# The second layer's weights converted during the first layer's last block, with new costs in the list that orders the instructions

## The chip, the cores and the metric

The kernel runs on one core of a Trainium2 chip. The metric is the time of one execution on the device in microseconds (us), the median of several runs. Five engines with queues of their own matter here: TensorE (PE in the profile; PEld is its loading of weights), VectorE (DVE), ScalarE (ACT), GpSimd (POOL) and SyncE (SP), which here does nothing but issue DMAs.

## The reference, cut to what matters

```python
scores = scale * np.matmul(q, k.transpose(0, 1, 3, 2))        # 4 x 8 heads, 576 x 576, head width 64
cum = np.cumsum(np.log(np.clip(f, 0.0001, 1.0)), axis=-1)
scores = np.where(causal, -1e9, scores + cum[:, :, :, None] - cum[:, :, None, :])
attn = softmax(scores)
x = (attn @ v).transpose(0, 2, 1, 3).reshape(2304, 512)
h = x @ moe_w_in                                              # 512 -> 2048
x = (h * np.clip(h + 3.0, 0.0, 6.0) / 6.0) @ moe_w_out        # 2048 -> 512
h = x @ moe2_w_in
g = np.where(h >= 1, h, np.where(h <= -1, 0.0, (h + 1) ** 2 / 4))
return (g @ moe2_w_out).astype(np.float32)
```

An attention with a decay, and two dense layers of width 2048 over 2304 tokens. The four weight matrices arrive as 64-bit floats.

## The kernel before

**Work.** Attention goes over 4 batches and pairs of heads, the first 256 queries of a batch first, then the other 320. For a tile of 128 queries, `u_scores` makes scores in PSUM (tile `sc`), `softmax` adds the decay and takes minimum and exponential (`dec`, `dm`, `prob`), `u_norm` divides, `u_trans` transposes the probabilities through TensorE (`pt`), `u_out` multiplies by the values (`av`). `av` uses half of TensorE's columns (the profile shows the tile 128\*64); its last chunk of keys has 64 rows only (64\*64). `dec` is loaded from `ncum` in DRAM into one of two buffers.

**Layers.** Both dense layers go over blocks of tokens: five of layer 1 (512, 512, 512, 256, 512 wide) and five of layer 2. A block has 16 steps, one for each chunk of 128 hidden units. A step is 12 matmuls of `hp` (`moe_h`, weights `w[0]`), the activation on ACT and DVE (`u`, `g`), and 12 matmuls of `o` (`moe_o`, weights `w[1]`), two steps later. 12, because operands are split into a rounded part and a rest, and three of the products are taken. Attention is interleaved with blocks 0 to 3 of layer 1; what a block needs of it must be done before the block. Block 4 of layer 1 (steps 64 to 79) is the first without attention.

**Weights.** A raw half chunk (512 KB, `wraw`, three buffers) is turned into 32-bit floats in the tile `wr` (two buffers) by one ACT and four DVE instructions (`w_split`, L431 to L442), then split into the rounded part and the rest (ACT and DVE) in a slot `w`. There are 9 slots for each of the two matrices, and 16 from step 64 on, when attention's buffers are free. Layer 1's chunks are split once, written to `wf` in DRAM (`w_keep`) and loaded again where they don't stay. Layer 2's chunks go another way: between steps 17 and 62 (`PRE`, by width) they are loaded raw, converted, and the float is written to `wf` by a DMA that POOL issues (L447); in block 4 it comes back by a load of 256 KB (L416) and only then is split.

**Order.** The program is written in one order, and `plan` replaces it: `graph` gives each instruction its dependences and a cost, `schedule` runs a list over them (the engine and instruction that can begin first goes first), and each engine gets its row. A DMA costs bytes over `bw`, plus fixed times. All loads and stores but POOL's share one queue on SP, in that row's order. The tile `wr` also holds the parts that block 5's inputs are added from (`part`, L806 to L809) and layer 2's output.

Of the kernel before, what the change touches and what calls it, by code (L numbers as in the profile page):

```python
# [42 lines left out]
LAG = 2  # L43
GO = 0
XT = 11
PRE = (17, 62)
WRAW = 3
AHEAD = 60000
LEAD = (1, 1, 1, 1, 1, 1)
# [44 lines left out]
def graph(nc, homes, follows, held=()):  # L94
# [95 lines left out]
    for k in range(n):  # L190
        if eng[k] == "PE":
            last = k
        elif last is not None and type(ops[k]).__name__ == "InstDMACopy":
            if any(x[0].startswith(held) for x in info[k][1]) if held else False:
                deps[k].add(last)

    DMA = "DMA"
    cost, late, kind = [0.0] * n, [0.0] * n, [""] * n
    for k, i in enumerate(ops):
        t, (ins, outs) = type(i).__name__, info[k]  # L200
        e = eng[k]
        o = outs[0] if outs else None
        m = max([x[4] for x in ins + outs] or [1])
        psum = any(x[5] for x in ins)
        if t == "InstDMACopy":
            parts = (o[2] - o[1]) if homes.get(o[0], ("", bass.MemoryType.DRAM))[1] != bass.MemoryType.DRAM else P
            cost[k] = 420 if e == "SP" else 1100
            late[k] = 4.0 * o[4] * parts
            kind[k] = DMA
        elif e == "PE":  # L210
            cols = o[4]
            if str(i.ins[0].dtype).endswith("float32r"):
                c = max(cols, 64) / 2.4 + 13
            elif "pt" == o[0][:2]:
                c = 109
            else:
                c = 1.7 * cols if "sc" == o[0][:2] else max(120, cols * 0.82)
            cost[k], late[k] = c, 172
        elif e == "Activation":
            late[k] = 30  # L220
            cost[k] = (200 + 0.7 * m if psum else 215 + 0.83 * m) - 95 + (190 if len(outs) > 1 else 0)
            late[k] = 95 + 34
        elif e == "DVE":
            if t == "InstCustomDveAnt":
                c = 165 + 1.0 * m + 85
            elif t == "InstTensorTensor" or psum or t == "InstTensorCopy":
                c = 160 + 1.04 * m
            elif t == "InstTensorScalarPtr" and len(ins) < 2:
                c = 155 + 0.52 * m
            elif t == "InstTensorScalarPtr":  # L230
                c = 160 + 1.04 * m
                if len([x for x in ins if x[4] > 1]) < 2:
                    c = 155 + 0.52 * m
# [7 lines left out]
    return dict(eng=eng, deps=deps, users=users, slots=slots, nuses=nuses, first=first,  # L241
                where={x: (h[0], h[2]) for x, h in homes.items()}, cost=cost, late=late, kind=kind), ops, sets


def schedule(g, bw=330.0, fixed=3000.0, small=150.0):
    n, eng = len(g["eng"]), g["eng"]
    succ, left = [[] for _ in range(n)], [len(d) for d in g["deps"]]
    for k, d in enumerate(g["deps"]):
# [28 lines left out]
            t, need[tag] = max(t, f[m]), m + 1  # L277
        return t

    server = 0.0  # L280
    for _ in range(n):
        best = None
        for e in engines:
            for k in avail[e]:
                t = when(k)
                if t is not None:
                    c = (max(t, free[e]), k)
                    if best is None or c < best:
# [43 lines left out]
def tile_kernel(  # L332
# [27 lines left out]
    def bank(name):  # L360
# [2 lines left out]
        return p.tile([P, 512], F32, tag="ps", name=name)  # L363

    att = pool("att", 2)

    x2d = [dram.tile([DM, NT if x == 0 else T1[0]], F32, name=f"x2d{x}") for x in range(2)]
    wf = [
        [dram.tile([P, 2, 4, P] if c < NCH else [P, 4, P], F32, name=f"wf{c}_{x}") for x in range(2)]
        for c in range(2 * NCH)  # L370
    ]
    ncum = dram.tile([B * H, S], F32, name="ncum")
    wsb = [[wpool.tile([P, 2, 4, P], F32R, name=f"w{x}_{s}") for s in range(SLOTS[x])] for x in range(2)]
# [33 lines left out]

    def w_load(kind, c, half, s):
        if kind == "raw":
            raw = att.tile([P, 4 * P, 2], I32, tag="wraw", name="wraw", bufs=WRAW)  # L410
            nc.sync.dma_start(out=raw, in_=w[c // NCH, c % NCH, :, 8 * P * half:8 * P * half + 8 * P])
            return raw
        if kind == "parts":
            nc.sync.dma_start(out=wsb[half][s].bitcast(F32), in_=wf[c][half])
        else:
            nc.sync.dma_start(out=wsb[half][s][:, 1].bitcast(F32), in_=wf[c][half])  # L416

    def w_split(kind, c, half, s, raw):
        if kind == "parts":
            return  # L420
# [15 lines left out]
        nc.vector.tensor_scalar(  # L436
            out=t, in0=t, scalar1=5, scalar2=2, op0=ALU.logical_shift_left, op1=ALU.logical_shift_right
        )
        nc.vector.scalar_tensor_tensor(  # L439
            out=t, in0=hw, scalar=-1073741824, in1=t, op0=ALU.bitwise_and, op1=ALU.bitwise_or  # L440
        )
        nc.vector.scalar_tensor_tensor(  # L442
            out=t, in0=lw, scalar=29, in1=t,
            op0=ALU.logical_shift_right, op1=ALU.bitwise_or,
        )
        if s is None:
            nc.gpsimd.dma_start(out=wf[c][half], in_=r)  # L447
        else:
            hi, lo = wsb[half][s][:, 0], wsb[half][s][:, 1]
            rounded("a", hi, r)  # L450
            rest("v", lo, r, hi)

    def w_keep(c, half, s):
        nc.sync.dma_start(out=wf[c][half], in_=wsb[half][s].bitcast(F32))
# [218 lines left out]
    def u_trans(n, x):  # L673
# [3 lines left out]
        pr = pairs[d["p"]]  # L677
        if "pt" not in pr:
            pr["pt"] = att.tile([P, 4, 2, S - QA], F32, tag="pt", name="pt", bufs=1)
            if pr["half"]:  # L680
                pr["pt4"] = att.tile([D, 2, W4], F32, tag="pt4", name="pt4", bufs=1)
        pt = pr["pt"]
        t = bank("pt")

# [27 lines left out]
            rounded("a", pt[:, :, :, QA:S - QA], t.rearrange("p (c h n) -> p c h n", c=4, h=2))  # L712
        else:
            tr(0, prob[4], 4 * P, D)
            rounded("a", pr["pt4"].rearrange("p h n -> p (h n)"), t[0:D, 0:P])

    def u_out(p):

# [387 lines left out]
```

## Time and profile before

| | |
|---|---|
| runs | 1041.9, 1036.1, 1035.82 us; median 1036.1 us |
| profiled execution | 1042.43 us, span 1040.7 us |
| mean granted clock of TensorE | 0.974 |
| busy: PE, DVE, ACT, POOL | 1002.5, 586.5, 527.0, 94.6 us |
| moved by DMA | 148.19 MB |

Busy times are unions of one engine's instructions. A busy PE can still run at the lower clock, 0.5 of the full one, or change between tile shapes. The profiled execution lies 0.6% above the median.

### The profile page before, as it was taken

How to read it: one execution, taken by the hardware profiler on the slowest of the kernel's cores; microseconds unless marked ns; L12 is line 12 of the kernel's file. 1: busy time of each engine (PE TensorE's matmuls, PEld its weight loads, DVE VectorE, ACT ScalarE, POOL GpSimd, SP SyncE). 2: the span in 40 equal slices, each digit the busy share in tenths (PEclk: the TensorE clock that was granted, in tenths of full speed). 3: DMA queues.
4: the chain of work that ended last, by engine and by line, in shares of the span. 5: the costliest groups of instructions: out<-in, count | busy, mean ns of one | idle time of the engine just before them, and what ended most of it. 6: DMA issues, size and time to landing. Idle time of an engine off the chain costs nothing.

```text
span 1040.7 us, 14773 instructions
## 1 busy us (share of the span) xinstructions
PE 1002.5 (96%) x5002; PEld 802.5 (77%) x5002; DVE 586.5 (56%) x1390; ACT 527.0 (51%) x1208; POOL 94.6 (9%) x223
## 2 busy tenths in 40 slices
PE   7889989999889999989899999999999999999998
PEld 5557767776667778768798888888888888888897
DVE  6889768899877765868654565423322322222232
ACT  5987656566655644756543444333333333333343
POOL 2111111111111110112010000101000000000000
PEclk7688989999999999999999999999999999999999
DMA  6665478867687897557958433201100100000010
GB/s 184 192 205 160 119 225 268 276 200 237 173 302 265 258 299 241 172 160 237 294 163 336 153 119 94 98 1 41 41 1 1 66 1 1 20 26 1 1 42 21
DMA packets 76364, 148.19 MB, mean 142 GB/s; under 512 B 12544, under 2 KB 35584, under 8 KB 76288
## 3 DMA queue, kind: packets, MB, share of 16 engines
q1 hardware_dynamic: 73728, 138.86, 42.6%
q0 software_dynamic: 2560, 8.39, 2.1%
q8 instruction: 39, 0.64, 0.2%
q14 instruction: 37, 0.30, 0.1%
HBM read 113.59 MB, written 33.63 MB: 141 GB/s over the span
## 4 chain that ended last, share of the span: by engine, by line
PE 80%; DMA 11%; DVE 4%; ACT 3%; issue 1%; SPq 0%; POOL 0%; DVEq 0%; POOLq 0%; ACTq 0%
PE hp L822 34%; PE o L872 19%; PE o L865 14%; DMA dec<-ncum 6%; DMA wraw<-in_w 4%; PE av L728 4%; PE pt L686 4%; PE sc L642 3%; PE sc L632 1%; DVE prob L593 1%; PE sc L617 1%; ACT prob L599 1%; DMA wf<-wr 1%; DVE wr L439 1%; ACT wr L431 0%
## 5 line engine op out<-in xcount | busy, mean ns | idle before, releaser
L822 PE MATMUL hp<-xt,w 128*128 128x512 f32 (+1 forms) x960 | 237.5, 383 | 1.7 <-DVE xt L386 0.6
L865 PE MATMUL o<-g,w 128*128 128x512 f32 (+1 forms) x960 | 233.7, 379 | 0.0
L822 PE MATMUL hp<-x,w 128*128 128x512 f32 (+1 forms) x960 | 210.0, 368 | 0.0
L872 PE MATMUL o<-w,g 128*128 128x512 f32 x864 | 209.2, 390 | 0.0
L822 PEld LDWEIGHTS hp<-x,w 128*128 128x128 f32 x960 | 169.3, 188 | 31.3
L822 PEld LDWEIGHTS hp<-xt,w 128*128 128x128 f32 x960 | 168.7, 193 | 31.8 <-issue 1.5
L865 PEld LDWEIGHTS o<-g,w 128*128 128x128 f32 x960 | 166.9, 190 | 28.3 <-issue 0.7
L872 PEld LDWEIGHTS o<-w,g 128*128 128x128 f32 x864 | 160.9, 188 | 33.2 <-ACT osb L887 0.7
L834 DVE SCALAR_TENSOR_TENSOR u<-hp,u 128x512 f32<-128x512 f32 (+1 forms) x80 | 51.1, 638 | 211.4 <-ACT u L833 211.1
L832 ACT ACTIVATE u<-hp 128x512 f32<-128x512 f32 (+1 forms) x80 | 44.4, 555 | 196.4 <-PE hp L822 196.4
L386 DVE TENSOR_TENSOR g<-u,g 128x512 fp32r<-128x512 f32 (+1 forms) x160 | 102.3, 640 | 69.2 <-PE o L872 35.0
L378 ACT ACTIVATE g<-u 128x512 fp32r<-128x512 f32 (+1 forms) x160 | 94.0, 589 | 77.2 <-DVE u L834 50.9
L599 ACT ACTIVATE prob<-prob,mx 128x128 f32<-128x128 f32 (+4 forms) x144 | 83.3, 579 | 54.5 <-DVE mx L593 54.1
L686 PE MATMUL pt<-ident,prob 128*128 128x128 f32 (+1 forms) x400 | 72.9, 297 | 17.1 <-DVE prob L671 13.3
L829 ACT ACTIVATE u<-hp 128x512 f32<-128x512 f32 (+1 forms) x80 | 44.3, 553 | 80.5 <-PE hp L822 80.0
L830 DVE SCALAR_TENSOR_TENSOR u<-u,hp 128x512 f32<-128x512 f32 (+1 forms) x80 | 50.4, 630 | 59.6 <-ACT u L829 59.2
L378 ACT ACTIVATE pt<-pt 128x512 f32<-128x512 f32 (+3 forms) x160 | 63.8, 434 | 34.1 <-PE pt L686 33.3
L686 PEld LDWEIGHTS pt<-ident,prob 128*128 128x128 f32 (+1 forms) x400 | 50.9, 149 | 36.3 <-DVE prob L671 15.4
L593 DVE CUSTOM_DVE_ANT_0 prob<-sc,dec 128x256 f32<-128x256 f32 (+1 forms) x112 | 58.6, 534 | 34.5 <-DMA dec<-ncum 15.2
L728 PE MATMUL av<-pt,vv 128*64 128x320 f32 (+3 forms) x448 | 59.6, 384 | 2.9 <-ACT pt L378 2.8
L728 PEld LDWEIGHTS av<-pt,vv 128*64 128x64 f32 (+1 forms) x448 | 28.7, 141 | 34.9 <-issue 10.1
L431 ACT ACTIVATE wr<-wraw 128x512 f32<-128x512 f32 x64 | 42.6, 667 | 18.6 <-DMA wraw<-in_w 14.1
(71 smaller groups left out, 899.5 us busy)
## 6 DMA issues: line engine op xcount, KB each, us to landing
wraw<-in_w SPq DMA_DIRECT2D x64, 512.0 KB, 7.2
w<-wf SPq DMA_DIRECT2D x40, 512.0 KB, 9.4
wf<-w SPq DMA_DIRECT2D x28, 512.0 KB, 6.8
dec<-ncum SPq DMA_DIRECT2D x45, 256.0 KB, 4.9
kraw<-in_k SPq DMA_DIRECT2D x64, 144.0 KB, 5.1
wf<-wr POOLq DMA_DIRECT2D x32, 256.0 KB, 5.6
w<-wf SPq DMA_DIRECT2D x32, 256.0 KB, 2.7
x2d<-osb SPq DMA_DIRECT2D x22, 256.0 KB, 6.5
```

Of the source, the lines that this page charges most:

```text
L378: nc.scalar.activation(out=out, in_=in_, func=AF.Copy)
L386: e.tensor_tensor(out=out, in0=in_, in1=hi.bitcast(F32), op=ALU.subtract)
L593: nc.vector.tensor_tensor_reduce(out=py[:, a:e], in0=s, in1=dc, scale=-0.125, scalar=mx[:, 2 * z:2 * z + 1] if x else 3.0e38, op0=ALU.add, ...
L599: nc.scalar.activation(out=py, in_=py, func=AF.Exp, scale=-1.0, bias=mx[:, 2 * z + x:2 * z + x + 1], accum_out=sm[:, z:z + 1],)
L686: nc.tensor.transpose(t[:nk, o:o + P], p[:, c:c + nk], ident)
L728: nc.tensor.matmul(t[y * D:(y + 1) * D, o:nq], lhsT=vv[:nk, y, c], rhs=rhs, start=c == 0, stop=c == nkc - 1,)
L822: nc.tensor.matmul(hp, lhsT=ws[:, a, k], rhs=x[:, bb, 0:w], start=(k == 0 and a == 0 and bb == 0), stop=(k == KD - 1 and bb == 1),)
L830: nc.vector.scalar_tensor_tensor(out=u, in0=u, scalar=6.0, in1=hp, op0=ALU.min, op1=ALU.mult)
L832: nc.scalar.activation(out=u, in_=hp, func=AF.Relu, bias=0.5, scale=0.5)
L834: nc.vector.scalar_tensor_tensor(out=u, in0=hp, scalar=1.0, in1=u, op0=ALU.max, op1=ALU.min)
L865: nc.tensor.matmul(o, lhsT=ws[:, a, k], rhs=gg[:, bb], start=(n and k % m == 0 and a == 0 and bb == 0), stop=(last and bb == 1 and k % m = ...
L872: nc.tensor.matmul(acc[j][k], lhsT=gg[:, bb, k * P:(k + 1) * P], rhs=ws[:, a].rearrange("p k n -> p (k n)"), start=(n and a == 0 and bb == ...
```

## The change

Layer 2's chunks no longer pass through DRAM. Their raw halves are loaded from step 65 on, two halves every two steps (`LATE`), at the latest two steps before use, into `wraw` buffers in the memory that attention left (`rawp`), and converted and split straight into freed slots. The 32 writes by POOL and the 32 loads of 256 KB are gone, and the "whole" split with them. Besides, `av`'s last chunk uses all 128 rows, with zeros in the padded rows of `pt4`. In the list, `av`'s matmuls of one bank are bound together (`group`), a change of tile shape on PE costs 95, `bw` is 280 instead of 330, and some costs differ.

```diff
-PRE = (17, 62)
+LATE = (1, 2.0, 2)
...
+    group, mode, begun = [-1] * n, [None] * n, {}
+    for k in range(n):
+        if eng[k] == "PE":
+            mode[k] = tuple(ops[k].tile_size)
+            name = info[k][1][0][0]
+            if name.startswith("av"):
+                begun.setdefault(name, []).append(k)
+    for line in begun.values():
+        for a, b in zip(line, line[1:]):
+            group[a] = b
+        deps[line[0]] = set().union(*(deps[k] for k in line)) - set(line)
...
-            cost[k] = 420 if e == "SP" else 1100
+            issues += e == "SP"
+            cost[k] = 1100 if e != "SP" else 420 if issues > 24 else 540
...
+            elif "av" == o[0][:2]:
+                c = max(cols / 0.6, 210) if not ops[k].tile_position[1] else 7
...
-                c = 165 + 1.0 * m + 85
+                c = 172 + 1.0 * m
...
-def schedule(g, bw=330.0, fixed=3000.0, small=150.0):
+def schedule(g, bw=280.0, fixed=3000.0, small=150.0):
...
+                if e == "PE" and bound >= 0 and k != bound:
+                    continue
...
+        if e == "PE":
+            free[e] += 95 if g["mode"][k] != last else 0
+            last, bound = g["mode"][k], g["group"][k]
...
-            raw = att.tile([P, 4 * P, 2], I32, tag="wraw", name="wraw", bufs=WRAW)
+            raw = rawp[0].tile([P, 4 * P, 2], I32, tag="wraw", name="wraw", bufs=WRAW)
...
-        if kind == "whole":
-            hi, lo = wsb[half][s][:, 0], wsb[half][s][:, 1]
-            rounded("a", hi, lo.bitcast(F32))
-            rest("v", lo, lo.bitcast(F32), hi)
...
-        if s is None:
-            nc.gpsimd.dma_start(out=wf[c][half], in_=r)
-        else:
-            hi, lo = wsb[half][s][:, 0], wsb[half][s][:, 1]
-            rounded("a", hi, r)
-            rest("v", lo, r, hi)
+        hi, lo = wsb[half][s][:, 0], wsb[half][s][:, 1]
+        rounded("a", hi, r)
+        rest("v", lo, r, hi)
...
+    pt4 = att.tile([P, 2, W4], F32, tag="pt4", name="pt4", bufs=1)
+    nc.gpsimd.memset(pt4, 0.0)
...
-                nk, rhs = (D, d["pt4"][:, y]) if c == 4 else (P, pt[:, c, y, o:nq])
+                rhs = pt4[:, y] if c == 4 else pt[:, c, y, o:nq]
...
-            wq.append((free, min(free + 4, need - 2), "whole", c, x, s))
+            t = max(free, g7 + LATE[0] + int(LATE[1] * (c - NCH)) + x)
+            t = min(t, need - LATE[2])
...
+            wq.append((max(t - 3, g7), t, "raw", c, x, s))
...
-    for n, c in enumerate(first):
-        x = part[PRE[0]] + (part[PRE[1]] - part[PRE[0]]) * n // NCH
-        t = [g for g in range(len(steps)) if part[g] <= x][-1]
-        wq += [(t - 3, t, "raw", c, half, None) for half in range(2)]
...
-            ext = pool("ext", 1, reuse_waits="tile")
+            ext = rawp[0] = pool("ext", 1, reuse_waits="tile")
```

On SP, at the start of block 3, where block 2's output is stored (the profile's chain has these raw loads at 490 us and this `dec` load at 497 us), before:

```order
L891 DMA x2d_78<-osb 128x512 x2
L411 DMA wraw<-in_w 128x1024 x2
L891 DMA x2d_78<-osb 128x512 x2
L414 DMA w_2_147<-wf_0_102 128x1024
L513 DMA kraw<-in_k 64x576 x2
L414 DMA w_0_154<-wf_1_99 128x1024
L493 DMA dec<-ncum 128x1x576
```

And now, up to the same `dec` load:

```order
L435 DMA w_1_114<-wf_0_100 128x1024
L902 DMA x2d_78<-osb 128x512 x3
L526 DMA kraw<-in_k 64x576
L902 DMA x2d_78<-osb 128x512
L526 DMA kraw<-in_k 64x576
L506 DMA dec<-ncum 128x1x576
```

The two raw loads are gone from before `dec`, and two of the reloads from `wf` have moved behind it.

On PE, at the end of attention, where block 4's first `hp` (128x512) begins, before:

```order
L822 MATMUL hp<-xt,w_6_151 128x512 x3
L728 MATMUL av<-pt,vv 64x320 x6
L728 MATMUL av<-pt,vv 64x192 x2
L728 MATMUL av<-pt_6393,vv 64x64 x2
L822 MATMUL hp<-xt,w_6_151 128x512 x9
```

And now:

```order
L833 MATMUL hp<-xt,w_5_118 128x256 x12
L739 MATMUL av<-pt,vv 64x320 x6
L739 MATMUL av<-pt,vv 64x192 x2
L739 MATMUL av<-pt_132,vv 64x64 x2
L876 MATMUL o_5610<-g,w_3_125 128x256 x6
L876 MATMUL o_5611<-g,w_3_125 128x256 x6
L833 MATMUL hp<-xt,w_6_119 128x256 x12
L876 MATMUL o_5610<-g,w_4_126 128x256 x6
L876 MATMUL o_5611<-g,w_4_126 128x256 x6
L833 MATMUL hp<-xt,w_6_119 128x512 x12
```

The last `av` stood inside block 4's first `hp`; now three groups of 12 matmuls of block 3 stand between the two.

On DVE, at the end of layer 2's first block (steps 94 and 95), before:

```order
L386 TENSOR_TENSOR g<-u,g 128x512
L386 TENSOR_TENSOR x_8007<-x_8007 128x512
L386 TENSOR_TENSOR x_8539<-x_8539 128x512
L386 TENSOR_TENSOR x_8543<-x_8543 128x512
L386 TENSOR_TENSOR x_8547<-x_8547 128x512
L834 SCALAR_TENSOR_TENSOR u<-hp,u 128x512
```

And now, up to the rest of chunk 15's first half (`w_15_6300`), which step 95's `hp` reads; L446 to L456 are the four conversions:

```order
L845 SCALAR_TENSOR_TENSOR u<-hp,u 128x512
L456 SCALAR_TENSOR_TENSOR wr<-wraw,wr 128x512
L446 TENSOR_SCALAR wr<-wr 128x512
L408 TENSOR_TENSOR g<-u,g 128x512
L408 TENSOR_TENSOR w_13_6305<-wr,w_13_6305 128x512
L450 TENSOR_SCALAR wr<-wr 128x512
L453 SCALAR_TENSOR_TENSOR wr<-wraw,wr 128x512
L845 SCALAR_TENSOR_TENSOR u<-hp,u 128x512
L456 SCALAR_TENSOR_TENSOR wr<-wraw,wr 128x512
L446 TENSOR_SCALAR wr<-wr 128x512
L408 TENSOR_TENSOR g<-u,g 128x512
L408 TENSOR_TENSOR w_15_6300<-wr,w_15_6300 128x512
```

Where DVE had only `u`, `g` and the next inputs, conversions now stand around each `u`. In block 4 the new order has four halves converted by step 72, then block 5's four `part` additions (which hold the two `wr` buffers), and the other 28 halves from step 77 on. In this row of DVE, from the last `part` to `w_15_6300`, stand 53 conversions of the L446 and L450 kind and 124 other instructions of 512 columns, 7 of them on block 6's and 7's inputs; 23 of the 177 read what the one before them wrote. On PE, the new order has 89 changes of tile shape where the old had 124.

## Rows read from the trace of the kernel before

**Rows 1.** By stretch: PE, PEld, DVE, ACT, POOL busy; PEclk, DMA share, GB/s.

```profile
130.00:225.00 95.00, 89.79 (x454) 69.74 (x453) 76.14 (x188) 59.76 (x145) 10.90 (x29) 0.96 0.80 249
225.00:435.00 210.00, 201.24 (x1009) 154.72 (x1010) 158.26 (x391) 118.94 (x284) 32.78 (x81) 0.99 0.75 240
...
312.00:442.00 130.00, 130.00 (x660) 100.77 (x658) 90.28 (x221) 72.26 (x173) 17.30 (x45) 1.00 0.77 248
...
435.00:546.00 111.00, 104.25 (x700) 88.07 (x695) 75.41 (x204) 63.11 (x163) 16.91 (x43) 0.98 0.70 218
...
557.50:650.00 92.50, 92.50 (x421) 77.08 (x420) 49.62 (x76) 41.08 (x71) 2.66 (x3) 1.00 0.50 167
650.00:738.00 88.00, 88.00 (x390) 72.88 (x389) 31.87 (x46) 30.93 (x50) 7.91 (x11) 1.00 0.14 48
```

**Rows 2.** Chain that ended last, by time, in block 4 (start, us, what).

```profile
626.95 2.72 PE hp L822 x12
```

**Rows 3.** Waits of PE, 225 to 557.5 us: total, times, longest.

```profile
PE pt L686 <- DVE prob L671: 6.9, 3, 3.3
PE pt L686 <- DVE mx L593: 3.0, 1, 3.0
PE sc L642 <- ACT pt L378: 2.7, 1, 2.7
```

**Rows 4.** The same chain, between 270 and 515 us.

```profile
273.75 6.16 DMA wf<-wr
...
433.85 12.80 DMA dec<-ncum
...
490.62 6.51 DMA wraw<-in_w
497.19 16.04 DMA dec<-ncum
```

**Rows 5.** DMA issues: count, KB each, median us to landing.

```profile
wraw<-in_w SPq DMA_DIRECT2D x64, 512.0 KB, 7.2
...
wf<-wr POOLq DMA_DIRECT2D x32, 256.0 KB, 5.6
...
x<-x2d SPq DMA_DIRECT2D x12, 256.0 KB, 4.1
```

**Rows 6.** The tile `wraw`: its loads' time to landing.

```profile
DMA to landing us min/median/max: 4.5/7.2/11.3
```

**Rows 7.** Groups by line and form: busy, mean ns | idle before.

```profile
L439 DVE SCALAR_TENSOR_TENSOR wr<-wraw,wr 128x512 int32<-128x512 int32 x64 | 44.5, 695 | 0.6
...
L442 DVE SCALAR_TENSOR_TENSOR wr<-wraw,wr 128x512 int32<-128x512 int32 x64 | 44.2, 691 | 0.4
...
L431 ACT ACTIVATE wr<-wraw 128x512 f32<-128x512 f32 x64 | 42.6, 667 | 18.6 <-DMA wraw<-in_w 14.1 <-DMA wf<-wr 3.5 <-DVE w L386 1.0
...
L436 DVE TENSOR_SCALAR wr<-wr 128x512 int32<-128x512 int32 x64 | 27.8, 435 | 0.6
...
L432 DVE TENSOR_SCALAR wr<-wr 128x512 f32<-128x512 f32 x64 | 27.7, 433 | 7.8 <-ACT wr L431 7.6
```

**Rows 8.** Timeline of PE around two `av` groups (start, us, what).

```profile
496.89 0.76 PE L728 MATMUL av<-pt,vv 128*64 128x320 f32 x4
...
499.76 1.22 PE L865 MATMUL o<-g,w 128*128 128x256 f32 x8
...
551.34 2.42 PE L728 MATMUL av<-pt,vv 128*64 128x320 f32 x20
...
553.70 5.74 PE L822 MATMUL hp<-xt,w 128*128 128x512 f32 x24
```

**Rows 9.** Timeline in block 4: DVE and POOL (start, us, what).

```profile
590.08 2.50 DVE L386 TENSOR_TENSOR w<-w 128x512 fp32r<-128x512 f32 x4
...
599.80 0.93 POOL L380 TENSOR_SCALAR x<-part 128x512 fp32r<-128x512 f32 x1 [10.37 <-PE o L865]
...
600.16 1.10 DVE L386 TENSOR_TENSOR w<-w 128x512 fp32r<-128x512 f32 x1
```

More of the change, by code (lines that the diff above doesn't have):

```diff
@@ L195, in graph @@
                 deps[k].add(last)
+    group, mode, begun = [-1] * n, [None] * n, {}
[9 more added lines that the diff above has]
+        deps[line[0]] = set().union(*(deps[k] for k in line)) - set(line)
     DMA = "DMA"
     cost, late, kind = [0.0] * n, [0.0] * n, [""] * n
+    issues = 0
     for k, i in enumerate(ops):
@@ L220, in graph @@
             late[k] = 30
-            cost[k] = (200 + 0.7 * m if psum else 215 + 0.83 * m) - 95 + (190 if len(outs) > 1 else 0)
+            cost[k] = (200 + 0.7 * m if psum else 215 + 0.83 * m) - 95 + (190 if len(outs) > 1 else 67 if len(ins) > 1 and "prob" == ins[0][0][:4] else 0)
             late[k] = 95 + 34
@@ L232, in graph @@
                 if len([x for x in ins if x[4] > 1]) < 2:
-                    c = 155 + 0.52 * m
+                    c = 215 + 0.52 * m
             else:
@@ L239, in graph @@
             late[k] = 60
-    return dict(eng=eng, deps=deps, users=users, slots=slots, nuses=nuses, first=first,
+    return dict(group=group, mode=mode, eng=eng, deps=deps, users=users, slots=slots, nuses=nuses, first=first,
                 where={x: (h[0], h[2]) for x, h in homes.items()}, cost=cost, late=late, kind=kind), ops, sets
-def schedule(g, bw=330.0, fixed=3000.0, small=150.0):
+def schedule(g, bw=280.0, fixed=3000.0, small=150.0):
     n, eng = len(g["eng"]), g["eng"]
@@ L278, in when @@
         return t
-    server = 0.0
+    server, last, bound = 0.0, None, -1
     for _ in range(n):
@@ L365, in tile_kernel @@
     att = pool("att", 2)
+    rawp = [att]
     x2d = [dram.tile([DM, NT if x == 0 else T1[0]], F32, name=f"x2d{x}") for x in range(2)]
     wf = [
-        [dram.tile([P, 2, 4, P] if c < NCH else [P, 4, P], F32, name=f"wf{c}_{x}") for x in range(2)]
-        for c in range(2 * NCH)
+        [dram.tile([P, 2, 4, P], F32, name=f"wf{c}_{x}") for x in range(2)]
+        for c in range(NCH)
     ]
@@ L409, in w_load @@
         if kind == "raw":
-            raw = att.tile([P, 4 * P, 2], I32, tag="wraw", name="wraw", bufs=WRAW)
+            raw = rawp[0].tile([P, 4 * P, 2], I32, tag="wraw", name="wraw", bufs=WRAW)
             nc.sync.dma_start(out=raw, in_=w[c // NCH, c % NCH, :, 8 * P * half:8 * P * half + 8 * P])
             return raw
-        if kind == "parts":
-            nc.sync.dma_start(out=wsb[half][s].bitcast(F32), in_=wf[c][half])
-        else:
-            nc.sync.dma_start(out=wsb[half][s][:, 1].bitcast(F32), in_=wf[c][half])
+        nc.sync.dma_start(out=wsb[half][s].bitcast(F32), in_=wf[c][half])
     def w_split(kind, c, half, s, raw):
         if kind == "parts":
-            return
-        if kind == "whole":
-            hi, lo = wsb[half][s][:, 0], wsb[half][s][:, 1]
-            rounded("a", hi, lo.bitcast(F32))
-            rest("v", lo, lo.bitcast(F32), hi)
             return
@@ L445, in w_split @@
         )
-        if s is None:
-            nc.gpsimd.dma_start(out=wf[c][half], in_=r)
-        else:
-            hi, lo = wsb[half][s][:, 0], wsb[half][s][:, 1]
-            rounded("a", hi, r)
-            rest("v", lo, r, hi)
+        hi, lo = wsb[half][s][:, 0], wsb[half][s][:, 1]
+        rounded("a", hi, r)
+        rest("v", lo, r, hi)
     def w_keep(c, half, s):
@@ L679, in u_trans @@
             pr["pt"] = att.tile([P, 4, 2, S - QA], F32, tag="pt", name="pt", bufs=1)
-            if pr["half"]:
-                pr["pt4"] = att.tile([D, 2, W4], F32, tag="pt4", name="pt4", bufs=1)
         pt = pr["pt"]
@@ L714, in u_trans @@
             tr(0, prob[4], 4 * P, D)
-            rounded("a", pr["pt4"].rearrange("p h n -> p (h n)"), t[0:D, 0:P])
+            rounded("a", pt4[0:D].rearrange("p h n -> p (h n)"), t[0:D, 0:P])
     def u_out(p):
@@ L726, in u_out @@
             for y in range(2):
-                nk, rhs = (D, d["pt4"][:, y]) if c == 4 else (P, pt[:, c, y, o:nq])
+                rhs = pt4[:, y] if c == 4 else pt[:, c, y, o:nq]
                 nc.tensor.matmul(
-                    t[y * D:(y + 1) * D, o:nq], lhsT=vv[:nk, y, c], rhs=rhs, start=c == 0, stop=c == nkc - 1,
+                    t[y * D:(y + 1) * D, o:nq], lhsT=vv[:, y, c], rhs=rhs, start=c == 0, stop=c == nkc - 1,
                 )
@@ L944, in tile_kernel @@
         if c >= NCH:
-            wq.append((free, min(free + 4, need - 2), "whole", c, x, s))
+            t = max(free, g7 + LATE[0] + int(LATE[1] * (c - NCH)) + x)
+            t = min(t, need - LATE[2])
+            assert t >= free, (c, x, free, need)
+            wq.append((max(t - 3, g7), t, "raw", c, x, s))
         elif (c, x) in seen:
@@ L951, in tile_kernel @@
             wq.append((t - 3, t, "raw", c, x, s))
-    first = list(dict.fromkeys(c for c, _, _, _, _ in loads if c >= NCH))
     span = [WIDTH[j] for j, _ in steps]
     part = [sum(span[:g]) for g in range(len(steps) + 1)]
-    for n, c in enumerate(first):
-        x = part[PRE[0]] + (part[PRE[1]] - part[PRE[0]]) * n // NCH
-        t = [g for g in range(len(steps)) if part[g] <= x][-1]
-        wq += [(t - 3, t, "raw", c, half, None) for half in range(2)]
     wq.sort(key=lambda x: x[0])
```

## Prediction

> **What bounds the kernel now.** First I read the busy times by stretch. From block 4 of layer 1 on, PE is busy in all of the time at the full clock [rows 1] (its two last rows), and the chain of waits is nothing but matmuls: 12 in 2.72 us, so a step of 24 takes 5.44 us [rows 2]. Nothing can be gained there; it can only be lost. Whatever the change brings must come from the part with attention. There PE stands still for 8.8 of 210 us and 6.8 of 111 us in the two stretches in which layer 2's chunks are converted (columns 1 and 2 of [rows 1]), and the granted clock, 0.99 and 0.98, costs another 2.1 and 2.2 us (one minus the clock, times the stretch). That is 15.5 + 4.3 = 19.8 us.
>
> Next, who ends these waits: three lines hold 12.6 of the 15.5 us, in five waits [rows 3]. They name DVE and ACT, but the same waits in the chain of time lead further back, to transfers: a `wf` write of POOL that took 6.2 us, `dec` loads of 12.8 and 16.0 us, and ahead of the last a raw load of 6.5 us on the same queue [rows 4]. So PE waits late in the softmax because `dec` lands late, and `dec` is late because the DMA engines are 0.75 and 0.70 busy in the mean [rows 1] and raw loads stand in front of it. The reader should see both: an engine is named, a transfer is meant.
>
> **The change, part by part.** The work is summed against the profiled execution, 1042.4 us (span 1040.7), which is 6.3 us above the median of the runs; I carry the differences over to the median, 1036.1.
>
> *Taken from attention's time.* 32 raw loads of 512 KB and 32 writes of 256 KB [rows 5] are 16.8 + 8.4 = 25.2 MB. The two stretches move 240 GB/s x 210 us + 218 x 111 = 74.6 MB [rows 1], so a third of the traffic goes. On DVE 32 x (433 + 435 + 695 + 691 ns) = 72.1 us go out of 233.7 us busy, on ACT 32 x 667 ns = 21.3 us [rows 1, 7], on POOL the 32 issues behind which the masks of `dec` stood. What is late next is the chunk reload from `wf`, which stays, and the softmax chain. The bounds are 0 (other transfers take the room) and 19.8 us. I take 70%, 13.9 us: the chain names a raw load, a `wf` write or a `dec` behind them for the waits that make up 12.6 of 15.5, and a third less traffic should not remove every one. That attention's last `av` moves to three groups of matmuls before block 4 in the new order agrees: it no longer holds up block 4.
>
> *Changes of tile shape.* 124 become 89 in PE's order. Price: an `av` group of 20 matmuls cut by one score matmul took from 496.89 to 499.76, 2.87 us, an uncut one from 551.34 to 553.70, 2.36 us [rows 8]. Less 0.17 us for the score matmul (384 columns, by 2.72 / 12 us for 512 [rows 2]), the two extra changes cost 0.34 us, 0.17 each. 35 x 0.17 = 6.0 us at the most, nothing where PE waits anyway. I take 3.5, because some of the changes lie where PE waits anyway. That `pt4` has 128 rows instead of 64 changes no count of columns; at nothing.
>
> *Added to block 4 and to layer 2's first block.* Layer 2's raw loads start behind the 14 reloads of 512 KB for block 4, and only four halves are converted by step 72: the two `wr` buffers then belong to block 5's `part` tiles until step 77, so nothing is converted for four and a half steps. The other 28 halves must pass DVE between step 77 and the first `hp` of step 95, 18 x 5.44 = 97.9 us. DVE has there, in the new order, 53 conversions of one operand and 124 other instructions of 512 columns. In a row without waits the latter follow each other at (2.50 - 0.69) / 3 = 0.60 us (four in 2.50 us, one alone 0.69) [rows 7, 9], the former I leave at their full 0.434: 23.0 + 74.8 = 97.8 us. DVE is thus as good as full, and step 95's weights come last of all. If every instruction took its full duration it would be 53 x 0.434 + 124 x 0.69 = 108.6 us, 10.7 too long; that, and 0, are the bounds. POOL converts seven of the next blocks' inputs in this time, and one such instruction held a DVE instruction from 0.69 to 1.10 us [rows 9]: 7 x 0.41 = 2.9 us. I take 3 us of PE waits, nearer to the row without waits, since only 23 of these 177 instructions read what the one before them wrote. Behind a DVE instruction that waits for a raw half are queued `u` and `g` of the running step, and PE waits for those within two steps. The first steps of layer 2 have slack: chunk 0 and 1 are done by step 72.
>
> The Trainium skill's page "SBUF — State Buffer", section "SBUF: two separate sides", says that a DVE instruction with two SBUF inputs and a GpSimd instruction share a pair of ports, and that whichever comes second stands still for the whole of the other. The row shows less, 0.41 us lost to a POOL instruction of 0.93 us. By the rule the seven would cost 7 x 0.93 = 6.5 us instead of 2.9; I follow the row.
>
> *Where the order is merely different.* The first 225 us have no layer 2 work, but the new costs shift instructions there too. In the last stretch of it, from 130 us, PE stands still for 5.2 us [rows 1], so it could be 5 us either way; I take 0.
>
> Sum: -13.9 - 3.5 + 3 = -14.4 us: 1028.0 for an execution like the profiled one, **1021.7 us for the median**, 1022.
>
> **The rivals.** *A, the waits stay.* `dec` is late because of reloads and attention's own loads, and the softmax chain is as long as before. For it: the 16.0 us landing of `dec` lies in a time in which reloads from `wf` are moved too, and those stay; and from 312 to 442 us PE stands still for 0 of 130 us at a DMA share of 0.77 [rows 1], so traffic alone makes no wait. Against it: 25.2 of 74.6 MB go, and in the chain a raw load or a `wf` write stands directly before the late `dec` or is the late transfer itself [rows 4]. With 20% of 19.8 us, 3.5 for shapes and 3 lost: 1036.1 - 4.0 - 3.5 + 3 = 1031.6 us.
>
> *B, all of it.* Every wait and low clock goes, the shapes give all 6.0, and DVE keeps up: 1036.1 - 25.8 = 1010.3 us.
>
> *C, the port.* POOL's conversions hold DVE for all of their 0.93 us, in the stretch where DVE is full: 6.5 instead of 2.9 us, and PE waits behind `u`: 1021.7 + 3.6 = 1025.3 us. This is what the Trainium skill's page on SBUF, named above, would make of it.
>
> *D, the ring of raw buffers (slower).* Three `wraw` buffers: a half holds one from its issue to the fourth conversion, landing + 0.667 (ACT) + 2.254 us (DVE) [rows 7]. At the median landing of 7.2 us that is 10.1, a third is 3.4 us for each half; 97.9 / 28 = 3.5 us are there. At the longest landing, 11.3 us [rows 6], it is 4.7 us a half, 28 x 4.74 = 132.7 us, 34.8 too long: 1036.1 - 17.4 + 34.8 = 1053.5 us. The kernel gets slower from a landing of 9.4 us on (17.4 us lost). Against it: the DMA share was 0.50 and 0.14 here, where most raw loads landed at 0.70 to 0.80; with 8.4 MB out and 16.8 MB in, 167 x 92.5 us + 48 x 88 us = 19.7 MB become 28 MB in 180 us, 155 GB/s against 240, and an input of 256 KB lands in 4.1 us [rows 1, 5].
>
> **How the numbers follow.** Forecast 0.47, A 0.25, B 0.12, C 0.08, D 0.08. The likeliest time is 1022. The range reaches from B's side, 1009, through A and the price of a DVE that takes its full durations (1021.7 + 7.7 = 1029.4) to 1035; D and a little of A and B stay out. A measurement of this kernel can tell about 1% from no change, that is 10.4 us, 1025.7 and 1046.5. Faster by more: 0.7 of the forecast, all of B, half of C, a tenth of A, 0.52. Slower by more: most of D, 0.06. Within 1%: 0.42.
>
> **What would show it.** Right: PE's busy share between 225 us and block 4 rises, waits of PE above 2 us with `dec` behind them get rarer, block 4 starts some 15 us earlier, DMA moves 148.2 - 16.8 = 131.4 MB (the writes and the loads of 256 KB gone). In layer 2's first block DVE is nearly full, and PE has a few waits for `w` near steps 92 to 95. D would show as ACT waiting for `wraw` and PE standing still from step 85 on; C as `x` instructions on POOL beside DVE instructions of over 1.2 us. What would make it wrong: the first 225 us going another way by more than 5 us, since I have put nothing there.

## The result, and the profile after

| | before | after |
|---|---|---|
| median | 1037.15 us (1035.82 to 1041.9, 4 runs) | 1024.74 us (1022.89 to 1025.11, 4 runs) |
| ratio | | 0.9869, 95% interval 0.9834 to 0.9904 |
| profiled execution, span | 1042.43, 1040.7 us | 1025.11, 1023.4 us |
| mean granted clock of TensorE | 0.974 | 0.978 |
| busy: PE, DVE, ACT, POOL | 1002.5, 586.5, 527.0, 94.6 us | 994.8, 588.0, 529.6, 73.0 us |
| moved by DMA | 148.19 MB | 131.39 MB |

The kernel became 1.3% faster. The profiled execution of before lies 5.3 us above its median, that of after 0.4 us, so the two profiles differ by 17.3 us where the medians differ by 12.4. First the busy times by stretch of the kernel after, with the columns of [rows 1]:

```profile
130.00:225.00 95.00, 92.72 (x476) 72.26 (x473) 75.59 (x183) 59.46 (x141) 11.49 (x31) 1.00 0.77 241
225.00:285.00 60.00, 53.48 (x262) 39.91 (x261) 44.79 (x114) 37.05 (x90) 4.56 (x18) 0.91 0.45 123
225.00:435.00 210.00, 202.12 (x1036) 157.03 (x1035) 126.07 (x333) 116.52 (x291) 18.61 (x66) 0.98 0.59 174
435.00:546.00 111.00, 110.88 (x751) 96.61 (x750) 52.99 (x145) 53.47 (x139) 6.43 (x24) 1.00 0.52 173
546.00:640.00 94.00, 94.00 (x416) 77.83 (x416) 64.68 (x114) 40.89 (x69) 4.65 (x5) 1.00 0.42 137
640.00:740.00 100.00, 99.51 (x438) 81.62 (x437) 81.56 (x141) 56.14 (x94) 9.88 (x11) 1.00 0.36 123
```

Against [rows 1] the DMA share falls from 0.75 to 0.59 and from 0.70 to 0.52 in the two stretches that held layer 2's conversions, and DVE's time in them from 233.7 to 179.1 us. In the second, PE now stands still for 0.1 us where it was 6.8. But in the first it still stands still for 7.9 of 210 us, against 8.8, at a lower clock, 0.98, than the 0.99 of before; 6.5 us of this and a clock of 0.91 lie in its first 60 us alone. The relief came in one stretch and not in the other, and that asks for a reason. By 225 us PE had begun 467 matmuls of `hp` and `o`, against 433 in the kernel before, and by 285 us 594 against 594: the changed kernel came into this stretch with a lead of some 34 x 0.227 = 7.7 us (2.72 us for 12 [rows 2]) and lost most of it there.

PE's waits from 225 to 557 us of the kernel after (in total, times, longest), beside [rows 3]:

```profile
PE pt L697 <- DVE mx L606: 3.0, 2, 2.0
PE pt L697 <- DVE prob L684: 2.5, 1, 2.5
PE o L876 <- DVE osb L900: 1.4, 1, 1.4
```

And the transfers in its chain of waits from 225 to 300 us, beside [rows 4]:

```profile
232.44 7.85 DMA kraw<-in_k
...
262.02 7.34 DMA kraw<-in_k
...
286.21 6.77 DMA x2d<-osb
```

Late `dec` loads and `wf` writes have left the chain, as the prediction wanted (from 300 to 560 us no transfer stands in it at all); two late `kraw` loads (attention's keys) stand there in their place. Behind them the softmax is late, and PE waits for `prob` and `mx` as before.

Then the part that the change loads. In pieces of 26 us, layer 2's first block of the kernel after:

```profile
624.00:650.00 26.00, 26.00 (x116) 21.54 (x115) 25.70 (x45) 15.76 (x28) 6.79 (x6) 1.00 0.72 242
650.00:676.00 26.00, 26.00 (x117) 21.52 (x116) 25.80 (x49) 17.24 (x29) 0.70 (x1) 1.00 0.38 125
676.00:702.00 26.00, 25.51 (x112) 20.41 (x111) 25.65 (x49) 17.95 (x30) 0.00 (x0) 1.00 0.49 162
```

DVE (third engine column) is busy for 77.15 of 78 us, and PE loses 0.49 us. The waits of PE from 546 to 740 us name the weights of the last steps, once each:

```profile
PE hp L833 <- ACT w L400: 0.3, 1, 0.3
PE hp L833 <- DVE w L408: 0.2, 1, 0.2
```

From the views of the tile `wraw` and of the line of POOL's conversions, for the same part (L453 is the conversion that was L439 in [rows 7]; duration min/median/max in ns):

```profile
L453 DVE SCALAR_TENSOR_TENSOR wr<-wraw,wr x32: 678/685/1093, 560.5 to 706.0; 128x512 int32<-128x512 int32 x32
...
DMA to landing us min/median/max: 3.7/3.9/5.9
```

```profile
L402 POOL TENSOR_SCALAR x<-x x11: 623/1046/2406, 638.3 to 710.7; 128x512 fp32r<-128x512 f32 x11
```

Layer 2's raw halves land in 3.9 us, half of the 7.2 us of [rows 5, 6]; both are medians of few landings, as the traces tell those of 6 of the 29 halves here and of 7 of the 64 before. Where POOL and DVE run side by side, both are held (in POOL's line, six of its conversions in a row):

```profile
638.33 6.79 POOL L402 TENSOR_SCALAR x<-x 128x512 fp32r<-128x512 f32 x6 [33.76 <-DMA x<-x2d]
...
642.54 1.08 DVE L408 TENSOR_TENSOR g<-u,g 128x512 fp32r<-128x512 f32 x1
643.55 1.09 DVE L453 SCALAR_TENSOR_TENSOR wr<-wraw,wr 128x512 int32<-128x512 int32 x1
```

The first of the six takes 2.41 us, while the DVE instructions beside it take their usual time; from 640.8 us on DVE's take 0.83 to 1.09 us, each 0.34 to 0.41 longer than elsewhere (0.42 and 0.69), and POOL's up to 1.06 where the shortest takes 0.62.

### The profile page after: what moved, and what is told of

Same layout as the page of the kernel before. It is cut to its first block, busy times and chain, and to the rows that moved or that the text cites. A ratio compares the mean times of both kernels' runs of the same rounds, so it can differ in the third digit from the quotient of the medians.

```text
span 1023.4 us, 14617 instructions
## 1 busy us (share of the span) xinstructions
PE 994.8 (97%) x5002; PEld 800.6 (78%) x5002; DVE 588.0 (57%) x1390; ACT 529.6 (52%) x1208; POOL 73.0 (7%) x192
## 2 busy tenths in 40 slices
DMA packets 69193, 131.39 MB, mean 128 GB/s; under 512 B 11520, under 2 KB 34560, under 8 KB 69120
## 4 chain that ended last, share of the span: by engine, by line
PE 80%; DVE 9%; DMA 6%; ACT 2%; issue 2%; SPq 0%; DVEq 0%; POOL 0%; ACTq 0%; POOLq 0%
PE hp L833 33%; PE o L876 17%; PE o L883 17%; PE av L739 4%; PE pt L697 4%; PE sc L655 3%; DMA wraw<-in_w 3%; DMA kraw<-in_k 2%; PE sc L630 2%; DVE wr L453 1%; DVE wr L456 1%; DVE w L408 1%; DVE prob L606 1%; ACT prob L612 1%; DVE wr L446 1%
## 5 line engine op out<-in xcount | busy, mean ns | idle before, releaser
L833 PE MATMUL hp<-xt,w 128*128 128x512 f32 (+1 forms) x960 | 232.6, 382 | 1.1 <-ACT xt L400 0.7
L876 PE MATMUL o<-g,w 128*128 128x512 f32 (+1 forms) x960 | 229.4, 378 | 1.4 <-DVE osb L900 1.4
L606 DVE CUSTOM_DVE_ANT_0 prob<-sc,dec 128x256 f32<-128x256 f32 (+1 forms) x112 | 58.6, 534 | 37.3 <-PE sc L655 22.5
L400 ACT ACTIVATE w<-wr 128x512 fp32r<-128x512 f32 x64 | 40.3, 629 | 28.8 <-DVE wr L456 28.5
L739 PE MATMUL av<-pt,vv 128*64 128x320 f32 (+3 forms) x448 | 53.7, 382 | 0.7 <-ACT pt L400 0.7
```

Source lines behind the costliest of these rows:

```text
L400: nc.scalar.activation(out=out, in_=in_, func=AF.Copy)
L606: nc.vector.tensor_tensor_reduce(out=py[:, a:e], in0=s, in1=dc, scale=-0.125, scalar=mx[:, 2 * z:2 * z + 1] if x else 3.0e38, op0=ALU.add, ...
L739: nc.tensor.matmul(t[y * D:(y + 1) * D, o:nq], lhsT=vv[:, y, c], rhs=rhs, start=c == 0, stop=c == nkc - 1,)
L833: nc.tensor.matmul(hp, lhsT=ws[:, a, k], rhs=x[:, bb, 0:w], start=(k == 0 and a == 0 and bb == 0), stop=(k == KD - 1 and bb == 1),)
L876: nc.tensor.matmul(o, lhsT=ws[:, a, k], rhs=gg[:, bb], start=(n and k % m == 0 and a == 0 and bb == 0), stop=(last and bb == 1 and k % m = ...
```

## The experiments

All ratios are to the kernel before, timed beside the runs. Runs 1 to 4, 5 to 8 and 9 to 12 are three series, in which before had medians of 1037.96, 1040.02 and 1037.87 us; so a difference between runs of two series, by medians or by ratios, is good to some 3 us, and both are given where they differ. "Weights" is the move of layer 2's chunks, "shapes" the 128 rows of `pt4` with the bound `av` groups and the price of a shape change, "list" the other new costs.

| run | what is new against before | median us | ratio [95%] |
|---|---|---|---|
| 1 | weights | 1015.44 | 0.9783 [0.9759, 0.9807] |
| 2 | list | 1061.52 | 1.0233 [1.0208, 1.0257] |
| 3 | shapes | 1040.29 | 1.0023 [1.0000, 1.0046] |
| 4 | shapes, list | 1058.23 | 1.0202 [1.0169, 1.0234] |
| 5 | weights, shapes | 1010.11 | 0.9716 [0.9691, 0.9741] |
| 6 | weights, list | 1029.40 | 0.9900 [0.9877, 0.9923] |
| 7 | weights, the list's DMA costs | 1026.19 | 0.9867 [0.9844, 0.9891] |
| 8 | weights, the list's DVE and ACT costs | 1016.66 | 0.9780 [0.9755, 0.9805] |
| 9 | as 5, `bw` 280 | 1019.23 | 0.9835 [0.9802, 0.9868] |
| 10 | as 5, dearer first issues | 1013.33 | 0.9778 [0.9745, 0.9811] |
| 11 | as 5, `bw` 380 | 1030.59 | 0.9948 [0.9928, 0.9969] |
| 12 | as 5, two raw buffers | 1027.48 | 0.9915 [0.9887, 0.9943] |

**Run 1, the weights alone.** Against the changed kernel:

```diff
-            issues += e == "SP"
-            cost[k] = 1100 if e != "SP" else 420 if issues > 24 else 540
+            cost[k] = 420 if e == "SP" else 1100
...
-                c = 172 + 1.0 * m
+                c = 165 + 1.0 * m + 85
...
-def schedule(g, bw=280.0, fixed=3000.0, small=150.0):
+def schedule(g, bw=330.0, fixed=3000.0, small=150.0):
...
-                if e == "PE" and bound >= 0 and k != bound:
-                    continue
...
-                rhs = pt4[:, y] if c == 4 else pt[:, c, y, o:nq]
+                nk, rhs = (D, d["pt4"][:, y]) if c == 4 else (P, pt[:, c, y, o:nq])
```

> Only layer 2's weights are moved; the list's costs and the shape of the last value matmul are as before. If the gain comes from relieving attention's time of 25.2 MB and 72 us of DVE, this alone gives most of it: 9 to 11 us less than before, about 1027 us. If the gain comes from the order that the new costs make, this alone gives under 4 us, 1033 us or more.

It gained 22.5 us, twice what was expected and more than the whole change. By stretch:

```profile
225.00:285.00 60.00, 57.54 (x305) 43.94 (x303) 41.85 (x108) 36.24 (x90) 5.14 (x20) 1.00 0.45 131
285.00:435.00 150.00, 149.75 (x781) 117.95 (x782) 82.00 (x221) 80.67 (x203) 12.76 (x48) 1.00 0.61 185
435.00:546.00 111.00, 110.95 (x749) 96.76 (x748) 53.70 (x146) 53.71 (x137) 6.36 (x22) 1.00 0.59 197
```

PE stands still for 2.8 us from 225 to 546 us at the full clock, where [rows 1] had 15.5 us and 4.3 us of clock: 17.0 of the 19.8 us are gained here.

**Runs 2, 3 and 4, the other parts without it.** Run 2 has the kernel before with the new costs, run 3 with `pt4`, the bound groups and the price of 95 for a shape change, run 4 with all of them; the weights still go through DRAM.

```diff
-                c = 165 + 1.0 * m + 85
+                c = 172 + 1.0 * m
...
-def schedule(g, bw=330.0, fixed=3000.0, small=150.0):
+def schedule(g, bw=280.0, fixed=3000.0, small=150.0):
```

> Only the costs of the list (280 GB/s, DMA issue, DVE and ACT costs) are new. Relief theory: within 3 us of before, 1034 to 1040. Order theory: 5 us or more faster, 1032 or less.

> Only the padded last chunk of keys, the bound value matmuls and the cost of a change of tile shape are new. Changes of shape at 0.1 to 0.17 us each: 3 to 6 us faster, about 1033. If PE's waits take it back: within 2 us of before.

> The changed kernel with layer 2's weights sent through DRAM as before; list and shapes are new. Relief theory: only the shapes' 3 to 4 us remain, 1033 us. Order theory: 1027 us or less, the weights' move then being worth little.

The list's costs alone cost 24 us, which neither expectation had, and run 4 misses both of its own too; the shapes alone gain nothing. In run 2, the busy times of two stretches, and below them PE's waits in the last:

```profile
285.00:435.00 150.00, 139.20 (x679) 104.75 (x678) 100.33 (x244) 74.62 (x181) 18.79 (x54) 0.95 0.77 252
...
546.00:640.00 94.00, 82.87 (x391) 63.99 (x390) 51.03 (x98) 40.16 (x82) 6.25 (x13) 0.96 0.58 200
```

```profile
PE sc L644 <- DVE kk L388: 6.3, 1, 6.3
PE pt L688 <- DVE prob L673: 1.4, 2, 1.1
```

PE stands still for 10.8 and 11.1 us there, with lower clocks beside it; in the kernel before, block 4 runs from 557.5 us on without a gap [rows 1]. In run 2's timeline of PE, attention's last pair has nothing of block 3 left to stand beside it:

```profile
549.39 0.40 PE L644 MATMUL sc<-kk,ql 128*128 128x512 f32 x1
556.10 0.66 PE L644 MATMUL sc<-kk,qh 128*128 128x384 f32 x1 [6.31 <-DVE kk L388]
```

For run 3 the waits of the whole execution suggest where the shapes' gain went: scores that wait for a buffer which ACT's copies of `pt` or the softmax still hold. PE's waits before `sc` come to 21.8 us, where the kernel before has 8.4, and those before `pt` to 11.7 instead of 16.9; but these are one execution each.

```profile
PE sc L663 <- ACT pt L397: 10.0, 7, 4.2
...
PE sc L638 <- DVE mx L614: 6.7, 2, 4.3
```

**Runs 5 and 6, weights with one of the two others.** Run 5 is the changed kernel with the list's old costs (the first three pieces of run 1's diff), run 6 the changed kernel without the shapes (its last two pieces).

> The changed kernel with all old costs but those of tile shape: weights moved, value matmuls padded and bound. The weights alone gave 1015.4 us, the whole change 1024.7, so something in it costs 9 us. If it is the costs of the list: 1012 to 1016, the fastest so far, the shapes giving their 3 us. If it is the binding: 1021 to 1026.

> Weights moved and the new costs, without padding, binding and cost of a change of shape. If the costs lose the 9 us: 1024 to 1028. If the binding does: 1013 to 1017.

Run 5, 1010.11 us, is the fastest of all, 2 us faster than expected, and beats both kernels. On the moved weights the shapes are worth 5.3 us by the medians and 7.0 by the ratios (run 1 to run 5), or 4.7 and 3.2 (run 6 to the changed kernel), and the list costs 14.0 and 12.1 us (run 1 to run 6) or 14.6 and 15.9 (run 5 to the changed kernel). On the moved weights the two are nearly independent of each other. The move itself is not independent of them: it is worth 22.5 us by itself, and by the medians 30.2 us with the shapes (run 3 to run 5), 32.1 with the list (run 2 to run 6) and 33.5 with both (run 4 to the changed kernel).

**Runs 7 and 8, the list in halves,** on run 1:

```diff
-            cost[k] = 420 if e == "SP" else 1100
+            issues += e == "SP"
+            cost[k] = 1100 if e != "SP" else 420 if issues > 24 else 540
...
-def schedule(g, bw=330.0, fixed=3000.0, small=150.0):
+def schedule(g, bw=280.0, fixed=3000.0, small=150.0):
```

for run 7, and the costs of DVE and ACT for run 8.

> Weights moved, and of the new costs only the DMA's (280 GB/s, 540 for the first 24 issues on SP). If it is they that lose: 1022 or more, with the loss before 285 us as in the changed kernel. If the engines' costs lose: 1013 to 1018.

> Weights moved, and of the new costs only those of DVE and ACT instructions. If they lose: 1022 or more. If the DMA's costs lose: 1013 to 1018. If both this and the run with the DMA's costs alone lie near 1015 while both together lose, it is no single cost but the order that happens to come out.

The costs of the DMAs take 10.8 us by the medians (8.7 by the ratios), those of the engines 1.2 (-0.3), which is nothing that can be told.

**Runs 9, 10 and 11, the DMA costs one at a time,** on run 5: `bw` 280, the first 24 issues at 540, and `bw` 380, away from the change.

```diff
-def schedule(g, bw=330.0, fixed=3000.0, small=150.0):
+def schedule(g, bw=380.0, fixed=3000.0, small=150.0):
```

> This is the version with the weights moved and the shapes changed and the list's old costs (1010.1 us), in which the list counts 280 GB/s for a DMA instead of 330, and nothing else. Theory (the new transfer price is what costs: it shifts raw loads and first attention steps in the first 285 us): it alone brings most of the 10.8 us that both DMA prices cost without the shapes, so 1017 to 1021 us, and PE's waits lie in 225 to 285 us. Rival 1 (the dearer issue of SP's first 24 DMAs is what costs): within 2 us of 1010.1. Rival 2 (any other price gives another order, and its time is chance): then this and a price of 380 GB/s both lie above 1010.1, with the waits at different places.

> The same version with SP's first 24 issues at 540 instead of 420 in the list, transfers at 330 GB/s. Theory (the transfer price): within 3 us of 1010.1. Rival 1 (the issue price): 1017 to 1021 us. Rival 2 (chance of the order): anything from 1008 to 1025, with no sum between this and the run at 280 GB/s that gives the 14.6 us of the whole list.

> The same version with 380 GB/s, away from the changed value. Theory (a slower transfer in the list costs, so a trend): 1005 to 1011 us, not slower than 1010.1. Rival 2 (chance of the order, of which the old costs are a lucky one): slower than 1010.1 by 3 us or more, with PE's waits before 285 us.

`bw` 280 took 9.1 us (12.3 by the ratios) of run 5's lead, the issues 3.2 (6.4), just outside the 3 us expected: so the price of a transfer is the larger part of the list's cost, as the theory had it. But the trend that it supposed fell: 380 took 20.5 us. Both sides of 330 are worse. Either each number makes another order and 330 a lucky one, or 330 is best because it is nearest to the rate that the transfers have: divided by the DMA share, the GB/s of [rows 1] come to 311 to 343, an estimate, with 280 and 380 outside. Three prices don't tell these two apart. The losses of runs 9 and 11 lie before 285 us; run 10's profiled execution, 1010.39 us and its fastest, shows none. Run 5's busy times from 225 to 285 us, then run 9's, then run 11's with the stretch ahead of it, where run 11 loses most (run 5 has 89.96 of 95 us there):

```profile
225.00:285.00 60.00, 58.50 (x313) 45.12 (x311) 41.41 (x109) 36.24 (x89) 4.96 (x19) 1.00 0.43 126
```

```profile
225.00:285.00 60.00, 55.03 (x286) 41.85 (x285) 46.87 (x121) 37.46 (x92) 4.55 (x18) 0.97 0.50 132
```

```profile
130.00:225.00 95.00, 81.68 (x389) 63.65 (x387) 69.46 (x168) 53.51 (x123) 7.64 (x27) 0.91 0.73 228
225.00:285.00 60.00, 55.56 (x280) 43.42 (x280) 41.21 (x109) 35.20 (x85) 6.92 (x21) 0.94 0.36 104
```

What stands apart in the orders is when layer 1's last raw half is issued. In the ten traces with moved weights (the third column is the last start of the raw loads before 300 us, the last one what `wr` and `w` on DVE and ACT, layer 1's conversions and splits, take of the chain from 225 to 285 us):

| kernel | `bw` | last raw issue of layer 1, us | PE busy, 225 to 285 us | clock there | conversions in the chain there, us |
|---|---|---|---|---|---|
| run 10 | 330 | 218.9 | 58.48 | 1.00 | 0 |
| run 5 | 330 | 221.4 | 58.50 | 1.00 | 0 |
| run 8 | 330 | 223.0 | 57.57 | 1.00 | 0 |
| run 12 | 330 | 223.5 | 58.37 | 1.00 | 0 |
| run 1 | 330 | 224.7 | 57.54 | 1.00 | 0 |
| run 11 | 380 | 230.2 | 55.56 | 0.94 | 4.9 |
| run 9 | 280 | 235.3 | 55.03 | 0.97 | 4.0 |
| after | 280 | 235.6 | 53.48 | 0.91 | 6.0 |
| run 7 | 280 | 239.7 | 53.86 | 0.91 | 8.3 |
| run 6 | 280 | 242.9 | 55.81 | 0.97 | 7.8 |

The two groups don't overlap, but they are also the groups of price, so the ten traces are no ten independent trials. Where the raw loads are through by 225 us, PE loses 1.5 to 2.5 us in the next 60; where some are issued later, it loses 4.2 to 6.5 us and clock. Run 9's chain has the same two late `kraw` loads as the changed kernel's:

```profile
233.16 8.11 DMA kraw<-in_k
...
261.02 8.06 DMA kraw<-in_k
```

How raw halves make them late can be read in the changed kernel's chain, where layer 1's conversions stand on DVE ahead of `kk`. `kraw` has one buffer, so its next load is issued when `kk` has read the last:

```profile
227.32 0.68 DVE wr L453
...
228.62 0.60 DVE wr L456
229.22 0.34 DVE wr L446
...
230.67 0.42 DVE wr L450
...
231.12 0.77 DVE kk L408
...
231.91 0.49 SPq L526
...
232.44 7.85 DMA kraw<-in_k
```

For the second `kraw` this is weaker: it is issued 26 us after the last raw load, behind the softmax of the pair before. And run 11's loss begins earlier than the others'. No run moved these raw loads alone, so this cause is argued from the chains and not shown; that the transfer prices make the loss, and where it lies, is shown.

**Run 12, two raw buffers for layer 2,** on run 5, against rival D:

```diff
-            raw = rawp[0].tile([P, 4 * P, 2], I32, tag="wraw", name="wraw", bufs=WRAW)
+            raw = rawp[0].tile([P, 4 * P, 2], I32, tag="wraw", name="wraw", bufs=WRAW if rawp[0] is att else 2)
```

> The same version with two buffers instead of three for the raw halves of layer 2. A half holds a buffer from its issue to its fourth conversion. Where landing is 3.9 us as in the changed kernel's layer 2's first block, that is 3.9 + 0.67 + 2.25 = 6.8 us, 3.4 us a half with two buffers against the 3.5 us that there are: theory (the ring is far from deciding with three, since loads land in half of the time that I took from the kernel before): 0 to 8 us above 1010.1, and ACT's waits for raw halves appear from about 570 us on. Rival (the ring of three was nearly short already): 20 us or more slower, with PE standing still before layer 2's last steps of its first block.

It lost 17.4 us by the medians (20.6 by the ratios), between the two expectations. Most of it lies in layer 2's first block (PE's order is the same as run 5's up to 620 us, SP's up to 528):

```profile
650.00:676.00 26.00, 23.94 (x103) 18.57 (x102) 22.20 (x40) 14.72 (x26) 0.00 (x0) 1.00 0.35 121
676.00:702.00 26.00, 19.73 (x75) 14.29 (x73) 18.31 (x34) 12.18 (x21) 0.00 (x0) 0.93 0.35 122
702.00:728.00 26.00, 23.92 (x97) 19.35 (x98) 20.56 (x35) 13.91 (x24) 2.89 (x4) 0.93 0.33 114
```

DVE is no longer full and PE stands still for 10.4 of 78 us. The waits of PE there name `g` first, the work of the running step that is queued behind the conversions, and `w` second; SP's timeline has 15 raw loads between 641.15 and 703.4 us, whose landing the tile's view gives (the trace tells it of three); what SP waited for in this time stands last:

```profile
PE o L882 <- ACT g L399: 6.9, 3, 3.4
PE o L882 <- ACT w L399: 2.7, 1, 2.7
```

```profile
641.15 62.59 SPq L432 DMA_DIRECT2D wraw<-in_w  x15
```

```profile
DMA to landing us min/median/max: 3.5/3.5/3.7
```

```profile
SPq L432 <- DVE wr L455: 63.7, 16, 6.5
```

That is 62.2 us for 14 halves, 4.44 us each. The ring sets this pace: SP waits 63.7 us for the fourth conversion, L455, before its raw loads. ACT, whose waits for raw halves were expected, waits for them 0.4 us. Each of the two raw buffers is held for 8.9 us, which is also the median in the trace, from issue to the end of the fourth conversion, of layer 2's last 28 halves: 3.5 for the landing and 5.4 for the conversions, not the 2.9 us that the sum of their durations gives, since `u`, `g` and the splits stand between them on DVE. With three buffers 8.9 / 3 = 3.0 us a half fits into the 3.5 us that there are; with two it doesn't.

## Why the prediction was right, and where only its sum was

The time, 1024.74 us against 1022, and the sign came out; but two of the four terms were mis-sized, in opposite directions, and that they nearly cancel is luck.

*Relief of attention's time, -13.9 us.* The mechanism was right, and the size, by itself, too small: run 1 gave -22.5 us, of which 17.0 us can be seen between 225 and 546 us, 86% of the bound where 70% was taken. The other 5.5 us are not assigned. The two profiled executions differ by more than the medians, 26.6 us, as that of before is a slow one; 4.9 us of this stand at the first store of layer 1's output already (145.76 and 140.94 us), ahead of the work on layer 2. Runs 5 and 12, whose order is the same there, differ by 2.6 us at the same place (142.41 and 144.99), so much of it can be chance of the one execution.

*Shapes, -3.5 us.* Right in size with the weights moved, -3.2 to -7.0 us. That it holds "nothing where PE waits anyway" was the point: with the old weights, run 3, nothing came. One part had been put at nothing and is not: the padded rows of `pt4`. An uncut `av` group is followed by the next matmul in 2.20 us where [rows 8] had 2.36, which in 16 groups of 20 makes some 2.6 us, an estimate:

```profile
528.09 2.28 PE L739 MATMUL av<-pt,vv 128*64 128x320 f32 x20
530.29 1.70 PE L876 MATMUL o<-g,w 128*128 128x256 f32 x12
```

*DVE full, +3 us.* The reading was right (DVE 77.15 of 78 us, the last weights late by 0.2 and 0.3 us); the loss was 0.5 us, and in run 5, whose DVE is as full (77.42 us from 604 to 682), it was nothing. No DVE instruction was held for all of a POOL instruction, as rival C wanted: none took over 1.1 us. DVE lost 2.3 us in all to the seven POOL conversions from 638 to 652 us, near the 2.9 that were worked out, and POOL's were held as much, 1.05 us in the median and 2.41 at the most against 0.62. The Trainium skill's page "SBUF — State Buffer", section "SBUF: two separate sides", has whichever of the two starts second stand still until the other is done. The rows agree with that in kind, as each is held by the other; and the prediction's 0.93 us for each was more than the rule says, since only what is left of the other instruction is waited for (0.57 us in [rows 9]).

*Order, 0, with 5 us either way.* This is the step that failed. The new costs were put at nothing, and they took 12.1 to 15.9 us with the moved weights (run 1 to run 6, run 5 to the changed kernel), mostly through the price of a transfer (runs 7 and 9), and the loss lies not before 225 us, where the prediction looked for such shifts, but mostly from 225 to 285 us: PE busy 53.48 us at a clock of 0.91 against run 5's 58.50 at 1.00, 5.0 us of waits and some 5.4 us of clock, of the 14.4 us between the two executions. The prediction treated the new costs as a way to write down the same order; they are an edit with a size of its own, as large as the change's purpose. Its own sign of being wrong, the first 225 us going another way by more than 5 us, came too, in the profiled executions: a lead of 7.7 us by 225 us, as said above, of which up to 5.3 can be chance of before's slow execution.

So -22.5, -5 and +14 stand where -13.9, -3.5 and 0 were put, and the 0.5 that stands where +3 was put is within the 14, since run 5 doesn't have it: -13.5 us, and -12.4 was measured. Rival A's time, 1031.6, was not reached, yet its picture is partly true of the stretch from 225 to 435 us, for another reason than it gave. Rival B, all of it, 1010.3 us, is what run 5 measured without the list's costs, and it has B's picture as well: PE stands still for 1.5 of 321 us from 225 us on, at the full clock. Rival D didn't come with three buffers, since the landing halved, but it was nearer than worked out: held for landing plus 5.4 us, three buffers decide from a landing of 3 x 3.5 - 5.4 = 5.1 us, an estimate from run 12; the longest that the trace tells of from 546 us on was 5.9.

As foretold, DMA moves 131.4 MB, block 4's first matmul starts 15.8 us earlier (534.71 us for 550.55), and layer 2's first block has its few waits in the last steps.

## What to carry to other kernels

When an edit comes with new numbers for a planner, split it before judging either: here the move of the weights was worth 22.5 us and the numbers took over half of it back, and transfer prices of 280, 330 and 380 gave 1019, 1010 and 1031 us, the best in the middle. New costs don't make a better order by themselves; time several, and look at what the good ones have in common, here that layer 1's raw loads were all issued by 225 us (whether that is the cause isn't shown). And count the hold of a ring buffer with everything that its consumer's queue puts between the steps: 5.4 us here, not 2.9.

## What was not expected of the hardware

Beside a DVE that is busy for 99% of the time, POOL's 512-column conversions took 1.05 us in the median and up to 2.41, the shortest 0.62, and DVE's instructions beside them were longer too, by 0.3 to 0.4 us. Raw halves of 512 KB landed in 3.9 us at a DMA share of 0.36 to 0.42, and in 7.2 us at 0.70 to 0.80 before. The share alone doesn't set this: in run 6 three raw halves landed in 3.6 to 4.5 us between 200 and 250 us at shares of 0.65 and 0.56, and in the changed kernel one that was issued behind block 4's reloads, at 540 us, took 11.3.
